# Top-k attention with an ELU network: the scores of a step in one burst over four PSUM banks, with small parts in the banks' corners

## The chip, the core and the metric

The kernel runs on one core of a Trainium2 chip. The metric is the device time of one execution in microseconds (us); lower is better. The engines that matter are TensorE (PE in the profile; PEld are its weight loads), VectorE (DVE), ScalarE (ACT), GpSimd (POOL) and SyncE (SP), which issues the loads and stores. PSUM, where TensorE writes its results, has eight banks of 512 float32 columns.

## The reference

Everything is float32. The shapes are 8 batches, 8 heads, 576 positions, head size 64; the network takes 4608 tokens of 512 values through 2048 hidden units.

```python
scores = scale * np.matmul(q, k.transpose(0, 1, 3, 2))
kth = np.partition(scores, -top_k, axis=-1)[..., -top_k:-top_k + 1]     # top_k = 32
scores = np.where(scores >= kth, scores, -1000000000.0)
attn = np.exp(scores - np.max(scores, axis=-1, keepdims=True))
attn = attn / (np.sum(attn, axis=-1, keepdims=True) + 1e-09)
x = np.matmul(attn, v)            # then (B, H, S, D) -> (B*S, H*D)
h = x @ w_in
g = np.where(h > 0.0, h, np.exp(np.minimum(h, 0.0)) - 1.0)
out = g @ w_out
```

## The kernel before

**Steps.** The attention is cut into 144 steps. A step takes two heads and one tile of 128 queries: 576 = 4 x 128 + 64, so four full tiles for each batch and pair of heads, and the last 64 queries of four heads together as a "rem" tile. The work of a step is spread over four passes of the main loop (line 617). At index n the loop computes the scores of step n + 2 (`scores`, L280), finds the 32 largest of each row of step n on VectorE (`select`, L322: MAX8 and MATCH_REPLACE8, in four parts with a `yield` after each), masks and exponentiates step n - 1 on ScalarE (`mask`, L345), scales it on GpSimd (`normalise`, L362), and transposes step n - 2 on TensorE (`turn`, L375: nine blocks of 128 columns, called as main with four, rest with one and other with four). When the tiles of a group (one, or a pair in most of the run) are transposed, `attend` (L397) multiplies by the values in the next index.

**Scores.** `scores(u, half)` computes half of the 576 keys (HS = 288) for both heads. Head i stands on partitions 64 i to 64 i + 63, so its matmul uses 64 of the 128 rows of TensorE's array. Both heads of one half go to two banks of `ps_sc`, a pool with one buffer, and one ScalarE activation (L297) moves the half to SBUF. The second half is computed later in the same index, with other work between.

**The last 64 keys.** The values of the last 64 positions of two heads share one chunk of 128 partitions (chunk 2 J of `vT`, J = 4). `attend` therefore takes 64 rows for its last chunk, and 128 rows for the four before. Its output has 64 columns of the array per head, so each pair of matmuls stands side by side. `transpose_qk` (L236) turns keys and queries by blocks of 128 positions, and at last the 64 that are left over, with three transposes of 64 rows (L257).

**The network.** `ffn_pieces` (L457) makes pieces: 16 `hidden` pieces for a block of one to three tiles of 128 tokens (L471, then Relu and Exp on ScalarE, L479 and L480, and the gate on VectorE, L451), and four `project` pieces for each tile (L489). `feed` (L577) is called four times in each index; it first puts the open gates on VectorE's list, and then as many pieces on TensorE's as a budget allows. The hidden results and the projections take turns in the pool `ps_f`, three buffers; the transposes and the attend results use `ps_t`, three buffers. With the two banks of `ps_sc` that is all of PSUM.

**Order.** From index 8 on (`tight`) the order of the program is the order in which TensorE, ScalarE, VectorE and GpSimd execute (L643). Before that a scheduler orders the instructions. Each engine takes its list in order and waits by semaphores. Dependences inside one PSUM tile are kept by bank: a write to any part of a bank waits for the reads of that bank which stand ahead of it.

Of the kernel before, what the change touches and what calls it, by code (L numbers as in the profile page):

```python
# [8 lines left out]
AF = mybir.ActivationFunctionType  # L9
ALU = mybir.AluOpType  # L10
FP32 = mybir.dt.float32
U32 = mybir.dt.uint32
I32 = mybir.dt.int32
PSUM = bass.MemoryType.PSUM
# [66 lines left out]
def kernel(  # L81
# [9 lines left out]
    nc = tc.nc  # L91
    P = nc.NUM_PARTITIONS
    B, H, S, D = q.shape
    dm, dff = moe_w_in.shape[0], moe_w_in.shape[1] // 2
    J = S // P
    JP = J * P
    R = S - JP
    HS = S // 2
# [5 lines left out]
    KEYS, QUERIES = R, R + S  # L104
    scale = 1.0 / float(D) ** 0.5
# [3 lines left out]
    def pool(name, bufs, **kw):  # L109
        return ctx.enter_context(tc.tile_pool(name=name, bufs=bufs, **kw))  # L110

    const = pool("const", 1)
    ldpool = pool("ld", 2)
    kvpool = pool("kv", 5)
    scpool = pool("sc", 5)
# [4 lines left out]
    fpool = pool("f", 2)  # L120
    opool = pool("o", 1)
    ps_sc = pool("ps_sc", 1, space=PSUM)
    ps_t = pool("ps_t", 3, space=PSUM)
    ps_f = pool("ps_f", 3, space=PSUM)
    late = {}
    raws = ExitStack()
    early = raws.enter_context(tc.tile_pool(name="early", bufs=1))
# [2 lines left out]
    ident = const.tile([P, P], FP32, tag="ident", name="ident")  # L130
# [78 lines left out]
    loaded, kqT, vT = {}, {}, {}  # L209

    def load_qk(b, hp):
        for name, src in (("k", k), ("q", q)):
            t = ldpool.tile([P, J + 1, 2, D], FP32, tag=name + "in", name=name + "in")
            for hh in range(2):
                nc.sync.dma_start(
                    t[:, 0:J, hh, :],
                    src[b, 2 * hp + hh, 0:JP, :].rearrange("(p j) d -> p j d", j=J),
                )
            nc.sync.dma_start(
                t[0:R, J, :, :],  # L220
                src[b, 2 * hp : 2 * hp + 2, JP:S, :].rearrange("h p d -> p h d"),
            )
            loaded[b, hp, name] = t

    def load_v(b, hp):
        t = kvpool.tile([P, 2 * J + 1, D], FP32, tag="vT", name="vT")
        for hh in range(2):
            h = 2 * hp + hh
            nc.sync.dma_start(
                t[:, hh * J : (hh + 1) * J, :],  # L230
                v[b, h, 0:JP, :].rearrange("(p j) d -> p j d", j=J),
            )
            nc.sync.dma_start(t[hh * R : (hh + 1) * R, 2 * J, :], v[b, h, JP:S, :])
        vT[b, hp] = t

    def transpose_qk(b, hp):  # L236

        d = kvpool.tile([P, 4 * J + 3, D], FP32, tag="kqT", name="kqT")
        kqT[b, hp] = d[:].rearrange("p c d -> p (c d)")
        srcs = [loaded.pop((b, hp, name)) for name in ("k", "q")]
        for i, src in enumerate(srcs):
            ps = ps_t.tile([P, JP], FP32, tag="t", name="qkps")
            for c in range(J):
                nc.tensor.transpose(  # L247
                    ps[:, c * P : (c + 1) * P],
                    src[:, c, :, :].rearrange("p h d -> p (h d)"),
                    ident[:],  # L250
                )
            c0 = KEYS + i * (2 * J + 1) * D
            nc.scalar.copy(kqT[b, hp][:, c0 : c0 + JP], ps[:])
            yield
        ps = ps_t.tile([P, JP], FP32, tag="t", name="qkps")
        for i, src in enumerate((srcs[0], *srcs)):
            nc.tensor.transpose(  # L257
                ps[:, i * R : (i + 1) * R],
                src[0:R, J, :, :].rearrange("p h d -> p (h d)"),
                ident[0:R, 0:R],  # L260
            )
        nc.scalar.copy(
            d[:, 0 : 4 * J + 3 : 2 * J + 1, :],
            ps[:, 0 : 3 * R].rearrange("p (a s) -> p a s", a=3),
        )
        yield

    def start_qk(b, hp):
        turning.append(transpose_qk(b, hp))
# [7 lines left out]

    turning = []

    def scores(u, half):  # L280

        if half == 0:
            u.sc = scpool.tile([P, 2, S], FP32, tag="sc", name="sc")
        ps = ps_sc.tile([P, 2, JP], FP32, tag="s", name="scps")
        q0 = QUERIES + u.t.qt * P
        for h, i, rows in u.heads:
            kq = kqT[u.t.b, h // 2]
            part = slice(i * D, (i + 1) * D)
            k0 = (KEYS if i == 0 else 0) + half * HS
            nc.tensor.matmul(  # L290
                ps[rows, i, 0:HS],
                kq[part, q0 : q0 + u.t.ql],
                kq[part, k0 : k0 + HS],
                start=True,
                stop=True,
            )
        nc.scalar.activation(  # L297
            u.sc[:, :, half * HS : (half + 1) * HS], ps[:, :, 0:HS], AF.Copy, scale=scale
        )

    def select_row(u, i):
        if i == 0:
# [72 lines left out]
    def turn(u, chunks):  # L375

        if u.turned:
            return
        g = u.group
        if g.et is None:  # L380
            g.et = etpool.tile([P, 2 * J + 1, len(g.tiles), P], FP32, tag="et", name="et")
        ps = ps_t.tile([P, JP], FP32, tag="t", name="eps")
        sc = u.sc[:, :, :].rearrange("p i s -> p (i s)")
        n = chunks.stop - chunks.start
        for c in range(n):
            c0 = (chunks.start + c) * P
            nc.tensor.transpose(ps[:, c * P : (c + 1) * P], sc[:, c0 : c0 + P], ident[:])  # L387
        nc.scalar.copy(  # L388
            g.et[:, chunks, u.at, :],
            ps[:, 0 : n * P].rearrange("p (c q) -> p c q", c=n),  # L390
        )
        if chunks.stop == 2 * J + 1:
            u.turned = True
            if u.at == len(g.tiles) - 1:
                closing.append(g)

    def attend(g):  # L397
        t = g.tiles[0]
        ps = ps_t.tile([P, JP], FP32, tag="t", name="avps")
        n = P if t.rem else sum(x.ql for x in g.tiles)  # L400
        for k in range(2 if t.rem else 1):
            hp = 2 * g.hp + k if t.rem else g.hp
            vt = vT[t.b, hp]
            for c in range(J + 1):
                for i in range(2):
                    rows = slice(0, P) if c < J else slice(i * R, (i + 1) * R)
                    chunk = J if c == J else i * (J + 1) + c
                    w = g.et[rows, chunk, :, :].rearrange("p a q -> p (a q)")
                    cols = slice(0, n)
                    if t.rem:  # L410
                        c0 = R * (k if i == 0 else 1 - k)
                        w = w[:, c0 : c0 + R]
                        cols = slice(k * R, (k + 1) * R)
                    nc.tensor.matmul(  # L414
                        ps[i * D : (i + 1) * D, cols],
                        vt[rows, 2 * J if c == J else i * J + c, :],
                        w,
                        start=(c == 0),
                        stop=(c == J),
                    )  # L420
        if t.rem:
            finish(t.block, 2, slice(2 * g.hp, 2 * g.hp + 2), t.cols,
                   ps[:, 0:n].rearrange("p (a q) -> p a q", a=2))
            return
        c0 = 0
        tiles = list(g.tiles)
        while tiles:
            blk, lo, parts = tiles[0].block, tiles[0].cols.start, 0
            while tiles and tiles[0].block is blk:
                parts += 1  # L430
                hi = tiles.pop(0).cols.stop
            finish(blk, parts, g.hp, slice(lo, hi), ps[:, c0 : c0 + hi - lo])
            c0 += hi - lo
# [161 lines left out]
    load_v(0, 0)  # L595
    start_qk(0, 0)
    turn_qk(True)
    scores(steps[0], 0)
    scores(steps[0], 1)
    load_qk(0, 2)  # L600
    start_qk(0, 1)
    turn_qk(True)
    scores(steps[1], 0)
    scores(steps[1], 1)
    load_qk(0, 3)
    for hp in range(1, NHP):
        load_v(0, hp)
# [7 lines left out]
    closing = []  # L615
    main, rest, other = slice(0, J), slice(J, J + 1), slice(J + 1, 2 * J + 1)
    for n in range(NS + 3):
# [2 lines left out]
        ahead, cur, prev, done = step(n + 2), step(n), step(n - 1), step(n - 2)  # L620
        if n < tight:
            turn_qk(True)
            scores(ahead, 0)
            scores(ahead, 1)
            for i in range(2):
                passes = select_row(cur, i)
                next(passes)
                if i == 0:
                    while closing:
                        attend(closing.pop(0))  # L630
                elif prev:
                    normalise(prev)
                    turn(prev, main)
                    turn(prev, rest)
                    turn(prev, other)
                feed(n, 0.25)
                next(passes)
                mask(cur, i)
                feed(n, 0.25)
            continue  # L640
# [4 lines left out]
            )  # L645
        passes = select(cur) if cur else iter(range(4))
        if ahead:
            scores(ahead, 0)
        next(passes)
        feed(n, 0.25)  # L650
        if prev:
            mask(prev, 0)
        turn_qk()
        while closing:
            attend(closing.pop(0))
        if ahead:
            scores(ahead, 1)
        next(passes)
        feed(n, 0.25)
        if done:  # L660
# [49 lines left out]
```

## Time and profile before

| what | value |
|---|---|
| median of 3 runs | 1733.86 us (1732.75 to 1734.05) |
| the profiled execution, its own time | 1732.9 us |
| its span, first to last instruction | 1731.0 us |
| granted TensorE clock, mean | 0.975 |
| busy: PE, DVE, ACT, POOL | 1647.5, 1544.7, 1145.1, 407.5 us |

The profile is read by stretch of time: the share of busy time of each engine in a stretch, what an engine waited for there, and the instructions in order of time with their start. PE's busy time is a union of records that overlap, and includes pauses inside a matmul's record; the distance from the start of one burst of matmuls to the start of the next tells more than the record's length. In the trace one float32 matmul has two MATMUL records (two passes), a transpose one. "128*64" in a row means 128 rows and 64 columns of the array in use, "128x256" the output's partitions and columns of the moving operand.

### The profile page before, as it was taken

How to read it: one execution, taken by the hardware profiler on the slowest of the kernel's cores; microseconds unless marked ns; L12 is line 12 of the kernel's file. 1: busy time of each engine (PE TensorE's matmuls, PEld its weight loads, DVE VectorE, ACT ScalarE, POOL GpSimd, SP SyncE). 2: the span in 40 equal slices, each digit the busy share in tenths (PEclk: the TensorE clock that was granted, in tenths of full speed). 3: DMA queues.
4: the chain of work that ended last, by engine and by line, in shares of the span. 5: the costliest groups of instructions: out<-in, count | busy, mean ns of one | idle time of the engine just before them, and what ended most of it. 6: DMA issues, size and time to landing. Idle time of an engine off the chain costs nothing.

```text
span 1731.0 us, 25867 instructions
## 1 busy us (share of the span) xinstructions
PE 1647.5 (95%) x8592; PEld 1007.8 (58%) x8592; DVE 1544.7 (89%) x3392; ACT 1145.1 (66%) x2509; POOL 407.5 (24%) x1078
## 2 busy tenths in 40 slices
PE   6468999999999999999999999999999999999999
PEld 3245677557474756555456565645547475745565
DVE  6899999999999999999989898999999989997700
ACT  5786787678676867667666675757657585756521
POOL 2674222222222222221212122221222221121100
PEclk9568999999999999999999999999999999999999
DMA  6641021001100110001200111001100000000000
GB/s 155 178 135 44 15 48 34 7 7 42 48 7 7 34 46 23 1 24 31 48 12 1 41 35 34 1 13 42 42 19 1 26 15 27 7 7 7 7 13 12
DMA packets 101125, 56.19 MB, mean 32 GB/s; under 512 B 84096, under 2 KB 92288, under 8 KB 100992
## 3 DMA queue, kind: packets, MB, share of 16 engines
q1 hardware_dynamic: 100992, 54.55, 11.5%
q8 instruction: 67, 1.10, 0.3%
q14 instruction: 66, 0.54, 0.1%
HBM read 45.09 MB, written 9.44 MB: 31 GB/s over the span
## 4 chain that ended last, share of the span: by engine, by line
PE 82%; DVE 8%; ACT 2%; issue 1%; POOL 1%; DMA 0%; ACTq 0%
PE ops L489 28%; PE hps L471 27%; PE avps L414 9%; PE scps L290 9%; PE eps L387 7%; DVE wk L334 3%; DVE m L341 3%; PE qkps L247 1%; DVE m L329 1%; ACT sc L297 1%; DVE gT L451 1%; PE qkps L257 0%; ACT n L480 0%; ACT n L479 0%; DVE wk L311 0%
## 5 line engine op out<-in xcount | busy, mean ns | idle before, releaser
L471 PE MATMUL hps<-xT,w_in 128*128 128x256 f32 (+2 forms) x2432 | 563.7, 378 | 22.8 <-DVE gT L451 15.6
L341 DVE MAX8 m<-wk 128x8 f32<-128x576 f32 x816 | 574.9, 745 | 0.0
L489 PE MATMUL ops<-w_out,gT 128*128 128x512 f32 x1152 | 525.3, 600 | 2.5 <-DVE gT L451 2.5
L471 PEld LDWEIGHTS hps<-xT,w_in 128*128 128x128 f32 x2432 | 406.1, 193 | 143.1 <-DVE gT L451 26.0
L334 DVE MATCH_REPLACE8 wk<-m,wk 128x576 f32<-128x576 f32 x544 | 399.4, 741 | 0.0
L489 PEld LDWEIGHTS ops<-w_out,gT 128*128 128x128 f32 x1152 | 208.7, 190 | 240.4 <-issue 232.5
L367 POOL TENSOR_SCALAR dene<-den 128x2 f32<-128x2 f32 x144 | 33.1, 230 | 1000.2 <-ACT sc L358 999.9
L290 PE MATMUL scps<-kqT 64*128 64x288 f32 (+1 forms) x1280 | 232.4, 462 | 32.6 <-ACT sc L297 24.3
L388 ACT COPY et<-eps 128x512 f32<-128x512 f32 (+1 forms) x432 | 189.8, 474 | 102.4 <-PE eps L387 102.3
L371 POOL TENSOR_SCALAR sc<-sc,rec 128x576 f32<-128x576 f32 x288 | 213.9, 752 | 185.1 <-DVE rec L369 175.2
L357 ACT ACTIVATE sc<-sc,neg 128x576 f32<-128x576 f32 x288 | 224.0, 778 | 48.4 <-POOL neg L354 48.1
L297 ACT ACTIVATE sc<-scps 128x576 f32<-128x576 f32 x288 | 185.9, 646 | 86.2 <-PE scps L290 81.4
L358 ACT ACTIVATE sc<-sc,gap 128x576 f32<-128x576 f32 x288 | 223.1, 775 | 25.3
L479 ACT ACTIVATE n<-hps 128x256 f32<-128x256 f32 (+2 forms) x304 | 111.5, 367 | 144.9 <-PE hps L471 131.9
L387 PEld LDWEIGHTS eps<-ident,sc 128*128 128x128 f32 x1296 | 156.8, 144 | 84.6 <-issue 53.9
L414 PE MATMUL avps<-et,vT 128*64 128x256 f32 (+5 forms) x2080 | 200.4, 328 | 3.8 <-ACT et L388 3.7
L387 PE MATMUL eps<-ident,sc 128*128 128x128 f32 x1296 | 192.1, 282 | 12.3 <-POOL sc L371 11.7
L334 DVE MATCH_REPLACE8 wk<-m,sc 128x576 f32<-128x576 f32 x272 | 199.7, 741 | 0.0
L329 DVE MAX8 m<-sc 128x8 f32<-128x576 f32 x272 | 191.1, 744 | 0.0
L451 DVE SCALAR_TENSOR_TENSOR gT<-n,hps 128x256 f32<-128x256 f32 (+2 forms) x304 | 117.6, 391 | 71.4 <-ACT n L480 70.7
L414 PEld LDWEIGHTS avps<-et,vT 128*64 128x64 f32 (+1 forms) x2080 | 115.4, 138 | 95.0 <-issue 53.8
L290 PEld LDWEIGHTS scps<-kqT 64*128 64x128 f32 (+1 forms) x1280 | 91.5, 180 | 126.0 <-issue 47.9
(40 smaller groups left out, 840.8 us busy)
## 6 DMA issues: line engine op xcount, KB each, us to landing
kin<-in_k_dram SPq DMA_DIRECT2D x64, 128.0 KB, 2.8
qin<-in_q_dram SPq DMA_DIRECT2D x64, 128.0 KB, 2.9
raw<-in_moe_w_in_dram SPq DMA_DIRECT2D x16, 512.0 KB, 4.1
vT<-in_v_dram SPq DMA_DIRECT2D x64, 128.0 KB, 2.3
raw<-in_moe_w_out_dram SPq DMA_DIRECT2D x16, 512.0 KB, 3.3
out_dram<-osb SPq DMA_DIRECT2D x32, 256.0 KB, 2.2
kin<-in_k_dram SPq DMA_DIRECT2D x32, 32.0 KB, 2.5
qin<-in_q_dram SPq DMA_DIRECT2D x32, 32.0 KB, 2.5
```

Source lines behind the costliest of these rows:

```text
L290: nc.tensor.matmul(ps[rows, i, 0:HS], kq[part, q0 : q0 + u.t.ql], kq[part, k0 : k0 + HS], start=True, stop=True,)
L297: nc.scalar.activation(u.sc[:, :, half * HS : (half + 1) * HS], ps[:, :, 0:HS], AF.Copy, scale=scale)
L329: nc.vector.max(found[i], cur[i])
L334: nc.vector.match_replace(wk[i], found[i], cur[i], TAKEN)
L341: nc.vector.max(found[i], cur[i])
L357: nc.scalar.activation(sc, sc, AF.Prelu, bias=neg[:], alpha=STEEP)
L358: nc.scalar.activation(sc, sc, AF.Exp, bias=gap[:], accum_out=u.den[:, i : i + 1])
L371: nc.gpsimd.tensor_scalar(u.sc[:, i, :], u.sc[:, i, :], rec[:, i : i + 1], 1.0, ALU.mult, ALU.mult)
L387: nc.tensor.transpose(ps[:, c * P : (c + 1) * P], sc[:, c0 : c0 + P], ident[:])
L414: nc.tensor.matmul(ps[i * D : (i + 1) * D, cols], vt[rows, 2 * J if c == J else i * J + c, :], w, start=(c == 0), stop=(c == J),)
L471: nc.tensor.matmul(ps[:, 0:n_tok], w_in[:, i, f * P : (f + 1) * P], blk.xT[:, i, 0:n_tok], start=(i == 0), stop=(i == NC - 1),)
L489: nc.tensor.matmul(blk.o[:], blk.gT[f // NG][:, f % NG, s * P : (s + 1) * P], w_out[:, f, :], start=(f == 0), stop=(f == NF - 1),)
```

## The change

`ps_sc` now holds one tile, `wide`, of four banks, allocated once. `ps_t` and `ps_f` go from three buffers to two. `scores(u)` issues the four matmuls of a step one after the other, head i and half h to bank 2 i + h, and then two activations, one for each head. In the banks' last 224 columns, which the scores leave free, stand the single block `rest` of `turn` (bank 3) and the left-over keys and queries (bank 1). The left-over 64 keys and 64 queries of two heads are loaded into one chunk of the `kin` tile, keys on partitions 0 to 63 and queries on 64 to 127; two transposes of all 128 rows, the second shifted by 64 columns, leave keys, keys and queries in 192 columns. They come first in `transpose_qk`. The last values of each head get a chunk of their own, with zeros (a GpSimd memset for each head) on the other head's partitions, so that `attend` takes 128 rows throughout. In the main loop `attend` stands right behind `scores`, ahead of the first `feed`.

```diff
-    ps_t = pool("ps_t", 3, space=PSUM)
-    ps_f = pool("ps_f", 3, space=PSUM)
+    ps_t = pool("ps_t", 2, space=PSUM)
+    ps_f = pool("ps_f", 2, space=PSUM)
+    wide = ps_sc.tile([P, 4, JP], FP32, tag="s", name="scps")
...
     def load_qk(b, hp):
...
-                t[0:R, J, :, :],
+                last[0:R, J, :, :] if name == "k" else last[R:P, J, :, :],
...
     def load_v(b, hp):
-        t = kvpool.tile([P, 2 * J + 1, D], FP32, tag="vT", name="vT")
+        t = kvpool.tile([P, 2 * J + 2, D], FP32, tag="vT", name="vT")
...
-            nc.sync.dma_start(t[hh * R : (hh + 1) * R, 2 * J, :], v[b, h, JP:S, :])
+            mine = slice(hh * R, (hh + 1) * R)
+            other = slice((1 - hh) * R, (2 - hh) * R)
+            nc.gpsimd.memset(t[other, 2 * J + hh, :], 0.0)
+            nc.sync.dma_start(t[mine, 2 * J + hh, :], v[b, h, JP:S, :])
...
     def transpose_qk(b, hp):
...
+        ps = wide[:, 1, HS : HS + 3 * R]
+        for i in range(2):
+            nc.tensor.transpose(
+                ps[:, i * R : i * R + P],
+                srcs[0][:, J, :, :].rearrange("p h d -> p (h d)"),
+                ident[:],
+            )
+        nc.scalar.copy(
+            d[:, 0 : 4 * J + 3 : 2 * J + 1, :],
+            ps.rearrange("p (a s) -> p a s", a=3),
+        )
         for i, src in enumerate(srcs):
...
-        for i, src in enumerate((srcs[0], *srcs)):
-            nc.tensor.transpose(
-                ps[:, i * R : (i + 1) * R],
-                src[0:R, J, :, :].rearrange("p h d -> p (h d)"),
-                ident[0:R, 0:R],
-            )
...
-    def scores(u, half):
+    def scores(u):
...
+        for half in range(2):
+            for h, i, rows in u.heads:
+                kq = kqT[u.t.b, h // 2]
+                part = slice(i * D, (i + 1) * D)
+                k0 = (KEYS if i == 0 else 0) + half * HS
+                nc.tensor.matmul(
+                    wide[rows, 2 * i + half, 0:HS],
+                    kq[part, q0 : q0 + u.t.ql],
+                    kq[part, k0 : k0 + HS],
+                    start=True,
+                    stop=True,
+                )
+        for i in range(2):
+            nc.scalar.activation(
+                u.sc[:, i, :].rearrange("p (a s) -> p a s", a=2),
+                wide[:, 2 * i : 2 * i + 2, 0:HS], AF.Copy, scale=scale,
+            )
...
     def turn(u, chunks):
-        ps = ps_t.tile([P, JP], FP32, tag="t", name="eps")
+        if chunks.stop - chunks.start == 1:
+            ps = wide[:, 3, HS : HS + P]
+        else:
+            ps = ps_t.tile([P, JP], FP32, tag="t", name="eps")
...
     def attend(g):
-                    rows = slice(0, P) if c < J else slice(i * R, (i + 1) * R)
-                    w = g.et[rows, chunk, :, :].rearrange("p a q -> p (a q)")
+                    w = g.et[:, chunk, :, :].rearrange("p a q -> p (a q)")
...
-                        vt[rows, 2 * J if c == J else i * J + c, :],
+                        vt[:, 2 * J + i if c == J else i * J + c, :],
...
         if ahead:
-            scores(ahead, 0)
+            scores(ahead)
+        while closing:
+            attend(closing.pop(0))
         next(passes)
         feed(n, 0.25)
         if prev:
             mask(prev, 0)
         turn_qk()
-        while closing:
-            attend(closing.pop(0))
-        if ahead:
-            scores(ahead, 1)
         next(passes)
```

More of the change, by code (lines that the diff above doesn't have):

```diff
@@ L212, in load_qk @@
         for name, src in (("k", k), ("q", q)):
-            t = ldpool.tile([P, J + 1, 2, D], FP32, tag=name + "in", name=name + "in")
+            n = J + 1 if name == "k" else J
+            t = ldpool.tile([P, n, 2, D], FP32, tag=name + "in", name=name + "in")
+            if name == "k":
+                last = t
             for hh in range(2):
@@ L254, in transpose_qk @@
             yield
-        ps = ps_t.tile([P, JP], FP32, tag="t", name="qkps")
-        for i, src in enumerate((srcs[0], *srcs)):
-            nc.tensor.transpose(
-                ps[:, i * R : (i + 1) * R],
-                src[0:R, J, :, :].rearrange("p h d -> p (h d)"),
-                ident[0:R, 0:R],
-            )
[L262 to L266, printed above, removed]
     def start_qk(b, hp):
@@ L278 @@
     turning = []
-    def scores(u, half):
-        if half == 0:
-            u.sc = scpool.tile([P, 2, S], FP32, tag="sc", name="sc")
-        ps = ps_sc.tile([P, 2, JP], FP32, tag="s", name="scps")
+    def scores(u):
+        u.sc = scpool.tile([P, 2, S], FP32, tag="sc", name="sc")
         q0 = QUERIES + u.t.qt * P
[L286 to L295, printed above, removed]
-            )
-        nc.scalar.activation(
-            u.sc[:, :, half * HS : (half + 1) * HS], ps[:, :, 0:HS], AF.Copy, scale=scale
-        )
+        for half in range(2):
[14 more added lines that the diff above has]
+                wide[:, 2 * i : 2 * i + 2, 0:HS], AF.Copy, scale=scale,
+            )
     def select_row(u, i):
@@ L597 @@
     turn_qk(True)
-    scores(steps[0], 0)
-    scores(steps[0], 1)
+    scores(steps[0])
     load_qk(0, 2)
@@ L602 @@
     turn_qk(True)
-    scores(steps[1], 0)
-    scores(steps[1], 1)
+    scores(steps[1])
     load_qk(0, 3)
@@ L647 @@
         if ahead:
-            scores(ahead, 0)
+            scores(ahead)
+        while closing:
+            attend(closing.pop(0))
         next(passes)
@@ L653 @@
         turn_qk()
-        while closing:
-            attend(closing.pop(0))
-        if ahead:
-            scores(ahead, 1)
         next(passes)
```

## The prediction

> **What bounds the kernel now.** I read busy time by stretch first, because an average over the span hides which engine leads where.
>
> ```profile
> core 0: us, PE busy (x) PEld busy (x) DVE busy (x) ACT busy (x) POOL busy (x), PEclk, DMA share, GB/s
> 200.00:400.00 200.00, 191.68 (x1341) 129.14 (x1341) 198.11 (x459) 145.34 (x351) 46.26 (x139) 1.00 0.10 26
> 400.00:600.00 200.00, 197.94 (x1009) 123.70 (x1006) 198.11 (x438) 143.63 (x313) 44.66 (x133) 1.00 0.11 27
> 600.00:800.00 200.00, 197.86 (x1062) 119.13 (x1060) 194.63 (x428) 136.76 (x296) 44.64 (x133) 1.00 0.09 25
> 800.00:1000.00 200.00, 199.79 (x953) 116.30 (x953) 186.55 (x409) 134.52 (x285) 42.34 (x127) 1.00 0.10 26
> 1636.00:1731.00 95.00, 91.07 (x320) 53.16 (x318) 7.07 (x18) 22.81 (x52) 3.82 (x9) 0.99 0.04 14
> ```
>
> Up to 600 us VectorE is busy 99% and bounds the kernel. From 800 us it is at 93% and TensorE at nearly 100%. After 1636 us only network work is left. Then what VectorE waited for, first from 200 to 600 us, then from 600 to 1636 us:
>
> ```profile
> DVE rec L369 <- POOL dene L367: 2.9, 4, 1.2
> DVE gT L451 <- ACT n L480: 0.9, 3, 0.5
> ```
>
> ```profile
> DVE rec L369 <- POOL dene L367: 44.9, 28, 3.9
> DVE gT L451 <- ACT n L480: 23.2, 26, 2.6
> ```
>
> So 3.8 us can be gained from 200 to 600, and at most 68 us after it. TensorE's own waits after 600 are small (the scores' wait for L297 is the largest, 6.5 us), so there TensorE executes its list without pause, and the list's length is the time. Third, TensorE's bursts in order of time (start, record length):
>
> ```profile
> 1019.70 1.89 PE L471 MATMUL hps<-xT,w_in 128*128 128x256 f32 x8
> 1021.52 0.76 PE L290 MATMUL scps<-kqT 64*128 64x288 f32 x4
> 1022.21 1.99 PE L471 MATMUL hps<-xT,w_in 128*128 128x256 f32 x8
> 1024.13 2.53 PE L414 MATMUL avps<-et,vT 128*64 128x256 f32 x20
> 1026.59 0.76 PE L290 MATMUL scps<-kqT 64*128 64x288 f32 x4
> 1027.28 1.99 PE L471 MATMUL hps<-xT,w_in 128*128 128x256 f32 x8
> 1029.11 1.15 PE L387 MATMUL eps<-ident,sc 128*128 128x128 f32 x9
> ```
>
> Read from start to start. Eight passes of 384 columns with no change around them run from 814.66 to 817.24 us, 0.84 us per 1000 columns: 0.215 for 256, 0.241 for 288; two passes on different rows or columns of the array run side by side. The score burst is two such pairs, 0.48, but takes 0.69. The hidden piece is 8 x 0.215 = 1.72, but takes 1.82 with a change of array shape at its end, 1.83 with one ahead of it, 1.92 with both. The attend burst (ten pairs, 2.15) takes 2.46 with a change ahead, one inside (its last four records are 64*64) and one at its end. So **each change of the rows or columns in use costs 0.093 us, and the first full-width matmul after it another 0.10 (0.05 for 64 columns)**, since the weights of the pass behind it aren't loaded ahead across the change.
>
> **What the Trainium skill says.** "TensorEngine Tiling (Array Packing)", Key Properties: changing the tiling mode drains TensorE. The trace agrees, with 0.093 us for the drain and the exposed weight load on top. "PSUM — Partial Sum Buffer", on bank collisions: TensorE's writes and another engine's reads are to be kept apart by bank and quadrant, even at different columns. So parts in a score bank's corner wait for that bank's activation, and the next scores for the corner's copy; no run here shows the corner. "TensorE: Matmul & The Clock Gate", Part 3: matmuls in different row groups run concurrently; the trace agrees (a pair of score passes starts 0.005 us apart).
>
> **The change part by part.**
>
> *Fewer shape changes.* I counted the places in TensorE's program order where the shape changes: 744 before, 384 after. An index with attend had six (into and out of the first half; into attend, into its 64-row chunk, into the second half, out); it now has three. One without had four, now two. The padded chunk costs no time: its pairs are still side by side at 0.215. Three transposes of 64 columns become two of 128: 0.17 to 0.22 us, 32 times, +1.6 in all. By stretch of 16 steps, from step 48 (its transposes begin at 590.7 us): 482 changes become 242. 240 x 0.093 = 22.3. The exposed weight loads fall from 35.4 to 20.7, so 14.7. Less 0.6 for the transposes: 36.4 us of TensorE's list, namely 6.8, 5.6, 7.4, 4.7, 6.9 for steps 48 to 127 and 5.0 for the rest. The same prices added up over the list before give 181.6 us for steps 80 to 95, and the trace has 180.7, so they hold. The 18 us saved ahead of step 48 are worth nothing: VectorE has 1 to 2 us in 200 to give.
>
> *How much of it arrives.* In steps 48 to 63 VectorE's waits (5.4 us idle from 600 to 800) let me count 4 of 6.8: **33.6**.
>
> *One burst instead of two halves.* The second half's wait for the single buffer goes: of the 6.5 us above I take **5**. In its place: the corner of bank 1, used directly behind the scores with no piece between in 4 of the 20 cases after step 48. It waits for the first activation, 0.65 (L297) plus ScalarE's usual delay of 0.05 to 0.4: **-4**. The corner of bank 3 comes at least 2.6 us behind the scores, both activations take 1.3: nothing, but up to 1.5 each where ScalarE is behind by a mask (0.78 + 0.78 + 0.19).
>
> *Attend earlier.* It now stands behind scores instead of behind scores and a piece, so it could meet the copy of "other" (L388). That copy ends 1.9 us (median, at most 2.9) after its transposes from 700 us on; attend comes 2.3 us or more after them. Nothing. But the first piece now has 2.3 us of attend ahead of it, and its gate is due one VectorE pass earlier than that of the piece which stood there (at 807.09 the gate waited 1.56 us). VectorE may fall back behind TensorE by up to about 1.9 us before GpSimd's scaling delays the transposes (in the index at 809.47, scaling ends at 812.14 and the transposes begin at 814.06), so I count little: as the two engines come within 3 to 4% of each other, **-6** (1 us per 16 steps, 0 to 15).
>
> *Two buffers for ps_f.* For each piece I compared its start with the end of the gate two allocations earlier. From 800 us on, three pieces in each 200 us start ahead of it, by 1.4 us in total: nothing. From 200 to 400 us, 30 of 57 do, by 37 us in total, since TensorE runs ahead there. That is idle time of TensorE, unless the piece's gate then comes late for VectorE. With the piece's own latency to the end of Exp (1.72 us for 128 columns, 2.77 for 256), ten gates from 110 to 400 us come late, by 3.4 us together: **-3.4**. If ScalarE's backlog stayed as it was, instead of absorbing the delay, it would be 13.2 from 200 to 400 and 30.8 before: 44 is the upper end.
>
> *The rest.* ps_t with two buffers: rest and left-over no longer use it. Copies end about 1 us after main, 1.9 after other, pieces of 1.8 us and more stand between: nothing. The 64 memsets (0.2 us each by the profile's one memset, 128x128) lie on GpSimd, 24% busy; those that wait for an attend stand an index or more behind it, and what queues behind them is neg and gap, due after a VectorE pass. Nothing, up to 2. At the start the first transposes now wait for the queries' tail (landing at 6.65 us, where keys began at 4.74), but ScalarE can't copy before 9.72, so nothing; with the scheduler's new order up to step 8, -5 to +5.
>
> Sum: 33.6 + 5 - 4 - 6 - 3.4 = 25.2. The span goes from 1731.0 to 1705.8. The profiled execution's own time is 1.9 above its span and 1.0 below the median shown: 1708.7, so **1709**.
>
> **Rivals.** *More arrives* (12%): VectorE keeps up without loss and no corner waits: 36.4 + 6.5 = 43, 1691. For it: VectorE had 68 us to give. Against: it is above 93% everywhere. *The gate takes the saving* (12%): VectorE can't fall back, so the 1.7 us that the first gate waits in an attend index come each time (45 after step 48); it then repeats what the later gate's 1.56 us cost before, and a gain of 0 to 8 stays: 1726 to 1734. Against: the 1.9 us of room. *Two gate buffers starve VectorE* (10%, the slower side): between 110 and 400 us, where VectorE bounds, each delayed piece hands its delay on. With 44 instead of 3.4: 25.2 - 40.6 = -15, 1749. It decides from 29 us lost there on. For it: a median margin of -0.14 us from 200 to 400. Against: the gates had 1.3 us of median slack behind Exp. That the change doesn't do what it says is excluded by the order of its instructions: four score matmuls stand together in every step.
>
> **Numbers.** Forecast 66%, own range 1698 to 1722. A measurement of this kernel tells 0.2% (3.5 us) from no change. Faster: 66 + 12 + 6 = 84%; within 0.2%: 4%; slower: 12%. The range reaches down into the first rival and up to the middle of the second: 1692 to 1729.
>
> **What would show it.** Right: from 800 us on VectorE's share at 96 to 97%, its wait for dene shrunk to a third; score bursts of about 1.17 us (0.10 + 4 x 0.241 + 0.09), attend 2.3; no 64*64 row at L414 for full tiles; index times as before up to 600 us. Wrong: gates waiting above 40 us for Exp after 600, TensorE waiting over 10 us for activations of the scores or for L451 there, or VectorE below 96% between 200 and 400 us.

## The result, and the profile after

The changed kernel takes 1747.97 us (median of 4 runs, 1745.18 to 1748.35) against 1733.53: ratio 1.008, 95% interval 1.0063 to 1.0098. It is slower by 14 us (0.8%); 1709 was predicted. Its profiled execution has a span of 1745.9 us. In the rows of the changed kernel L297 is the scores' matmul and L305 their activation, L255 and L260 the left-over keys' transposes and their copy, L399 the transposes of `turn`, L425 `attend`, and L482, L491 and L462 the hidden piece, its Exp and its gate.

Busy time by stretch of the changed kernel, with the columns of the table before:

```profile
core 0: us, PE busy (x) PEld busy (x) DVE busy (x) ACT busy (x) POOL busy (x), PEclk, DMA share, GB/s
200.00:400.00 200.00, 178.58 (x1275) 123.92 (x1274) 186.82 (x429) 136.35 (x333) 43.71 (x135) 0.99 0.09 24
400.00:600.00 200.00, 186.16 (x940) 121.06 (x938) 192.10 (x424) 136.59 (x296) 45.60 (x140) 1.00 0.09 24
600.00:800.00 200.00, 191.93 (x1109) 124.58 (x1110) 195.71 (x433) 138.96 (x305) 45.83 (x141) 1.00 0.10 27
800.00:1000.00 200.00, 194.09 (x913) 116.46 (x913) 188.83 (x412) 132.63 (x279) 43.48 (x134) 1.00 0.09 24
```

Up to 600 us neither engine is full any more: VectorE fell from 99% to 93 and 96%, TensorE too. After 800 us TensorE has idle time (97%), and VectorE is at 94%, hardly above the 93% of before. What VectorE waited for in the changed kernel, from 200 to 600 us and then from 600 to 1636 (total, times, longest), and TensorE's waits in the second stretch:

```profile
DVE gT L462 <- ACT n L491: 14.1, 22, 2.1
DVE rec L378 <- POOL dene L376: 6.9, 5, 1.8
```

```profile
DVE gT L462 <- ACT n L491: 31.3, 39, 2.3
DVE rec L378 <- POOL dene L376: 28.8, 18, 3.1
```

```profile
PE hps L482 <- DVE gT L462: 15.7, 25, 1.8
PE scps L399 <- ACT kqT L260: 8.7, 5, 2.0
PE scps L255 <- ACT sc L305: 5.3, 4, 1.4
```

Where VectorE bounds, its waits rose from 3.8 to 21.0 us. Where TensorE bounds, three waits are new, 29.7 us together: a piece for a gate, the rest block for the copy of the left-over keys, and the left-over keys for the scores' activation. The wait of 6.5 us that the scores had for their single buffer is gone. The start of each step's selection dates the loss: step 16 begins 3.4 us later than before (234.0 against 230.6), step 48 20.1 us later (583.9 against 563.8), and the last selection ends 13.7 us later (1649.4 against 1635.7). So 20 us are lost ahead of step 48, and of the 28.6 us expected behind it (33.6 + 5 - 4 - 6) 6.4 arrive.

The bursts themselves came out as worked out. TensorE's list in order of time (start, record length):

```profile
1042.56 1.24 PE L297 MATMUL scps<-kqT 64*128 64x288 f32 x8
1043.73 2.38 PE L425 MATMUL avps<-et,vT 128*64 128x256 f32 x20
1046.04 3.72 PE L482 MATMUL hps<-xT,w_in 128*128 128x256 f32 x16
```

From start to start the scores take 1.17 us and attend 2.31, as the prediction's last part has them.

### The profile page after: what moved, and what is told of

It is laid out like the page before. It is cut to its first block, busy times and chain, and to the rows that moved or that the text cites. A ratio compares the mean times of both kernels' runs of the same rounds, so it can differ in the third digit from the quotient of the medians.

```text
span 1745.9 us, 26194 instructions
## 1 busy us (share of the span) xinstructions
PE 1603.1 (92%) x8560; PEld 1030.3 (59%) x8560; DVE 1546.0 (89%) x3392; ACT 1142.8 (65%) x2509; POOL 416.6 (24%) x1142
## 3 DMA queue, kind: packets, MB, share of 16 engines
q1 hardware_dynamic: 100992, 54.55, 11.3%
## 4 chain that ended last, share of the span: by engine, by line
PE 62%; DVE 26%; ACT 6%; issue 3%; POOL 2%; DMA 1%; SPq 0%; ACTq 0%; POOLq 0%
PE ops L500 25%; PE hps L482 17%; DVE wk L343 10%; DVE m L350 8%; PE avps L425 8%; PE scps L297 6%; PE eps L399 4%; DVE m L338 2%; DVE gT L462 2%; ACT sc L366 1%; ACT sc L367 1%; DVE m L326 1%; DVE wk L320 1%; PE qkps L267 1%; ACT n L491 1%
## 5 line engine op out<-in xcount | busy, mean ns | idle before, releaser
L482 PE MATMUL hps<-xT,w_in 128*128 128x256 f32 (+2 forms) x2432 | 563.3, 380 | 69.4 <-DVE gT L462 60.4
L482 PEld LDWEIGHTS hps<-xT,w_in 128*128 128x128 f32 x2432 | 411.2, 194 | 182.5 <-DVE gT L462 87.4
L305 ACT ACTIVATE sc<-scps 128x576 f32<-128x576 f32 x288 | 171.6, 647 | 99.2 <-PE scps L297 98.1
L400 ACT COPY et<-eps 128x512 f32<-128x512 f32 x288 | 165.1, 573 | 90.5 <-PE eps L399 90.4
L462 DVE SCALAR_TENSOR_TENSOR gT<-n,hps 128x256 f32<-128x256 f32 (+2 forms) x304 | 119.1, 395 | 95.7 <-ACT n L491 95.7
L425 PE MATMUL avps<-et,vT 128*64 128x256 f32 (+2 forms) x2080 | 186.6, 324 | 12.7 <-ACT et L400 12.5
L297 PE MATMUL scps<-kqT 64*128 64x288 f32 (+1 forms) x1280 | 187.4, 442 | 9.0 <-ACT kqT L273 4.6
L399 PEld LDWEIGHTS eps<-ident,sc 128*128 128x128 f32 x1152 | 145.5, 145 | 80.4 <-issue 51.3
L399 PE MATMUL eps<-ident,sc 128*128 128x128 f32 x1152 | 177.4, 280 | 13.3 <-POOL sc L380 13.2
L425 PEld LDWEIGHTS avps<-et,vT 128*64 128x64 f32 x2080 | 119.1, 140 | 84.0 <-issue 29.9
L297 PEld LDWEIGHTS scps<-kqT 64*128 64x128 f32 (+1 forms) x1280 | 100.9, 183 | 74.6 <-issue 29.9
```

Source lines behind the costliest of these rows:

```text
L297: nc.tensor.matmul(wide[rows, 2 * i + half, 0:HS], kq[part, q0 : q0 + u.t.ql], kq[part, k0 : k0 + HS], start=True, stop=True,)
L305: nc.scalar.activation(u.sc[:, i, :].rearrange("p (a s) -> p a s", a=2), wide[:, 2 * i : 2 * i + 2, 0:HS], AF.Copy, scale=scale,)
L425: nc.tensor.matmul(ps[i * D : (i + 1) * D, cols], vt[:, 2 * J + i if c == J else i * J + c, :], w, start=(c == 0), stop=(c == J),)
L482: nc.tensor.matmul(ps[:, 0:n_tok], w_in[:, i, f * P : (f + 1) * P], blk.xT[:, i, 0:n_tok], start=(i == 0), stop=(i == NC - 1),)
```

## The experiments

**Two buffers for the gates alone**, in the kernel before.

```diff
-    ps_f = pool("ps_f", 3, space=PSUM)
+    ps_f = pool("ps_f", 2, space=PSUM)
```

> The kernel before with two buffers instead of three for the hidden and projection results (ps_f), nothing else. Theory of the buffers (TensorE's pieces wait for VectorE's gate two pieces back, and the next gate then comes late for VectorE): 1748 to 1760 us, slower by 14 us or more, with VectorE waiting more than 10 us for Exp between 200 and 600 us where it waited 0.9. Theory of the early attend (two buffers cost little, the moved attend is what makes gates late): within 5 us of 1733.5.

Measured: 1761.04 us, ratio 1.0158 (1.0143 to 1.0174), 27 us slower. From index 8 on TensorE's program order is unchanged, so this is waiting alone. VectorE's wait for Exp from 200 to 600 us rose from 0.9 to 6.5 us, less than the 10 expected, that for dene from 2.9 to 7.5. Step 48 begins 16.0 us later than before (579.8 against 563.8); the other 10.9 us up to the last selection are lost behind it. How a wait comes about, TensorE and then VectorE of this run:

```profile
300.85 1.16 PE L471 MATMUL hps<-xT,w_in 128*128 128x128 f32 x8 [0.23 <-DVE gT L451]
301.84 0.60 PE L387 MATMUL eps<-ident,sc 128*128 128x128 f32 x4
302.28 1.06 PE L471 MATMUL hps<-xT,w_in 128*128 128x128 f32 x8
304.14 1.16 PE L471 MATMUL hps<-xT,w_in 128*128 128x128 f32 x8 [0.80 <-DVE gT L451]
305.23 0.76 PE L290 MATMUL scps<-kqT 64*128 64x288 f32 x4
```

```profile
303.81 0.27 DVE L451 SCALAR_TENSOR_TENSOR gT<-n,hps 128x128 f32<-128x128 f32 x1
304.00 1.42 DVE L329 MAX8 m<-sc 128x8 f32<-128x576 f32 x2
305.33 0.27 DVE L451 SCALAR_TENSOR_TENSOR gT<-n,hps 128x128 f32<-128x128 f32 x1
305.99 0.29 DVE L451 SCALAR_TENSOR_TENSOR gT<-n,hps 128x128 f32<-128x128 f32 x1 [0.39 <-ACT n L480]
```

The piece at 304.14 needs the buffer of the piece at 300.85, whose gate VectorE reaches at 303.81, behind its MAX8 and MATCH_REPLACE8. TensorE idles 0.80, the scores behind the piece start later as well, and VectorE then waits 0.39 at 305.99 for that piece's own Exp. A wait for dene comes by a longer way, here with lines left out between:

```profile
279.69 0.76 ACT L388 COPY et<-eps 128x512 f32<-128x512 f32 x2 [3.40 <-PE eps L387]
281.20 0.77 ACT L358 ACTIVATE sc<-sc,gap 128x576 f32<-128x576 f32 x1
282.42 0.17 DVE L369 RECIPROCAL rec<-dene 128x2 f32<-128x2 f32 x1 [1.37 <-POOL dene L367]
```

ScalarE stands 3.40 us for TensorE's transposes; only behind their copies come the two masks, whose sums dene needs, and VectorE stands 1.37 us for it. The kernel before has such waits too; what the missing buffer adds is the rise from 2.9 to 7.5. The theory of the buffers stands.

**Two buffers for the transposes alone** (`ps_t` 3 to 2, kernel before).

> The kernel before with two buffers instead of three for transposes and attend results (ps_t), nothing else. Here rest and the left-over keys still use this pool, which the changed kernel takes out of it. Both theories: 1733 to 1740 us; the copies end one to two us after their transposes and further work stands between. If it is 10 us slower or more, neither theory is complete.

Measured: 1782.79 us, ratio 1.0282 (1.0267 to 1.0298): 49 us slower, a miss. TensorE's waits from 600 us on have a row that neither the kernel before nor the changed one has:

```profile
PE eps L387 <- ACT et L388: 21.4, 31, 1.1
```

Main, rest and other follow each other in this pool; with two buffers, other waits for main's copy. With the 5.2 us from 200 to 600 the row comes to 26.6 us; what makes up the rest of the 49 I did not follow. In the changed kernel rest stands in a corner and the row is absent, so this isn't its loss. It suggests what the corners are good for; two buffers without corners in the changed kernel were not run.

**Attend earlier alone.**

```diff
         if ahead:
             scores(ahead, 0)
+        while closing:
+            attend(closing.pop(0))
         next(passes)
...
         turn_qk()
-        while closing:
-            attend(closing.pop(0))
         if ahead:
             scores(ahead, 1)
```

> The kernel before with attend moved directly behind the first half of the scores, ahead of the first piece; all buffers as before. Theory of the early attend: slower by 10 us or more, with VectorE's wait for Exp well above the 24 us of before. Theory of the buffers: the same as before or a little faster (one shape change fewer in an index with attend, some 45 times after 600 us at 0.2 us: up to 9 us), 1724 to 1735 us.

Measured: 1752.38 us, ratio 1.011 (1.0093 to 1.0127), 18 us slower with all buffers as before. The sign and size are those of the theory of the attend, but VectorE's wait for Exp rises only between 200 and 600 us (0.9 to 8.2); after 600 its wait for dene rises (45.2 to 51.4). An index of this run from the first stretch, TensorE and then VectorE:

```profile
489.28 2.53 PE L414 MATMUL avps<-et,vT 128*64 128x256 f32 x20
491.74 1.99 PE L471 MATMUL hps<-xT,w_in 128*128 128x256 f32 x8
```

```profile
491.36 1.41 DVE L341 MAX8 m<-wk 128x8 f32<-128x576 f32 x2
494.63 0.42 DVE L451 SCALAR_TENSOR_TENSOR gT<-n,hps 128x256 f32<-128x256 f32 x1 [1.86 <-ACT n L480]
```

The first piece starts only at 491.74, behind attend's 2.46 us. Its gate is due behind the second pass, at 492.77, and starts at 494.63: VectorE stands for 1.86 us. Attend itself also met the copy of "other": TensorE waited there for L388, 4.3 us from 200 to 600 and 2.6 after, where the kernel before has no such wait from 200 us on. Step 48 begins 9.0 us later than before (572.8 against 563.8), and the stretch from there to the last selection is 8.6 us longer. Both theories are right, each about one part.

**The padded values alone.** The changed lines of `load_v` and `attend`, kernel before.

> The kernel before with the padded last values alone (no 64-row chunk in attend). Both theories: the shape change inside the attend burst goes (about 0.15 us, of which TensorE bounds some 45 bursts after 600 us), the burst takes 2.3 instead of 2.46 us: 1725 to 1731 us.

Measured: 1719.72 us, ratio 0.992 (0.9906 to 0.9935), 14 us faster, more than expected: both theories had counted too few changes. The trace has 637 in place of 744, and 72 of the 107 lie from step 48 to the last selection. At 0.093 + 0.05 each they are worth 10.3 us there, and that stretch is 10.4 us shorter (1061.5 against 1071.9). So the price of a shape change holds. 3.8 us of the gain stand at step 48 already (560.0 against 563.8), where the prediction had nothing; 2.5 of them come ahead of step 16.

**Attend put back in the changed kernel** (behind `turn_qk()`).

> The changed kernel with attend put back to its old place behind the first piece and the key transposes; all else as changed. If the costs of the parts add (two gate buffers +27 and early attend +18 us, each measured alone), it falls by 18 us less 56 more shape changes (some 8 us): 1735 to 1742 us. If the two gate buffers alone set the time and the place of attend matters only with three: 1746 to 1752 us.

Measured: 1723.48 us, ratio to before 0.9948 (0.9933 to 0.9963): 24.5 us faster than the changed kernel, and faster than either theory had it (18 less 8 was the larger gain expected), although the list has 56 shape changes more.

**The gate's buffer freed by ScalarE**, in the changed kernel; the copy stands ahead of the Exp, and `fpool` has three buffers.

```diff
-            gates.append((blk.gT[f // NG][:, f % NG, 0:n_tok], n, ps))
+            dst = blk.gT[f // NG][:, f % NG, 0:n_tok]
+            nc.scalar.copy(dst, ps[:, 0:n_tok])
+            gates.append((dst, n, dst))
```

> The changed kernel with the hidden results copied by ScalarE from PSUM into the gate's own place in SBUF, where the gate then works in place, and a third buffer for the Exp values: a PSUM buffer comes free behind ScalarE and no longer behind VectorE's gate. ScalarE gets 304 copies of about 0.37 us, 112 us more on 65%. Theory of the buffers: 1748 less about 27, 1716 to 1730 us, and TensorE's wait for the gate is gone. Theory that attend's place alone costs: 1743 us or more.

Measured: 1718.56 us, ratio 0.9914 (0.9898 to 0.9931): 29 us faster than the changed kernel. After 600 us TensorE's wait for a buffer of ps_f falls from 15.7 to 0.2 us; between 200 and 600 it falls from 25.8 to 11.3, now for ScalarE's copy, so there it is not gone. A third buffer of ps_f, which would be the plain test, does not fit beside the four score banks. VectorE's gates did not become faster: the 304 take 130.9 us in all, 120.1 in the changed kernel.

**Both repairs.**

> The changed kernel with both: hidden results copied by ScalarE, and attend at its old place. If the two causes are all that stands against the shorter list of TensorE: 1700 to 1715 us, near the 1709 of the prediction. If a further cause is missing (corners, ScalarE's load): above 1720 us.

Measured: 1706.18 us, ratio 0.9846 (0.9832 to 0.9861), within the expected range. That this is near the predicted 1709 is luck and no proof of the prediction's sum: with attend back this kernel has 56 shape changes more than the changed one, and the experiment with the score banks, further down, shows a further cause.

**The first half moved next to attend** (kernel before with padding; in an index with attend `scores(ahead, 0)` and attend stand behind `mask(prev, 0)`, and `turn_qk()` behind the second half).

> The kernel before with the padded values and, in an index with attend, the first half of the scores moved behind the first piece so that attend stands between the two halves (halves, buffers and corners as before): one shape change fewer in each such index than with padding alone (637 to 605). If only TensorE's list counts: 1713 to 1718 us against 1719.7 of padding alone. If moving work past a piece delays VectorE as the early attend did: 1722 us or more.

Measured: 1772.26 us, ratio 1.0225 (1.021 to 1.024): 53 us slower than padding alone, for 32 shape changes saved. TensorE's waits after 600 us show why; with padding alone this row has 6.5 us (from 200 to 600 it has 24.0 here and 2.2 there):

```profile
PE scps L293 <- ACT sc L300: 34.8, 41, 2.4
```

The first half's activation now stands behind the mask's two activations on ScalarE's list, and the second half waits for it.

**The score banks as two tiles**, on top of both repairs; the other changed lines only follow the new names:

```diff
-    wide = ps_sc.tile([P, 4, JP], FP32, tag="s", name="scps")
+    wide = [ps_sc.tile([P, 2, JP], FP32, tag=f"s{i}", name=f"scps{i}") for i in range(2)]
```

> As the changed kernel with hidden results copied by ScalarE and attend at its old place, and the score banks as two tiles of two banks, one for each head, so that the rest block (bank 3) need not wait for the left-over keys' copy (bank 1). There TensorE waited 4.4 us for that copy after 600 us, and 4.0 between 200 and 600. If that wait is on the path: 1700 to 1704 us against 1706.2; if VectorE's room hides it: 1705 to 1708.

Measured: 1694.44 us, ratio 0.9779 (0.9764 to 0.9793), 12 us faster than with the repairs alone, more than the 2 to 6 expected, and the fastest version here. VectorE's waits from 200 to 600 us, from 600 to 1636, and TensorE's largest wait in the second stretch:

```profile
DVE rec L380 <- POOL dene L378: 2.2, 1, 2.2
DVE gT L464 <- ACT n L495: 1.0, 2, 0.6
```

```profile
DVE rec L380 <- POOL dene L378: 27.8, 13, 13.6
DVE gT L464 <- ACT n L495: 13.3, 18, 2.0
```

```profile
PE scps L257 <- ACT sc L307: 2.2, 3, 0.7
```

The rest block's wait for the left-over keys' copy is gone, though the two stood in different banks before as well. The left-over keys' own wait fell too, from 5.2 to 2.2 us after 600. In one tile each of these waits was 1.3 us there and ended when the activations of both heads had ended; in two tiles it is 0.74 and ends with the first head's, which alone reads bank 1. The section on the kernel says that dependences inside a tile are kept by bank; for the wide tile that was not so in either place: the wait went by the whole tile. VectorE's waits after 600 us are 41.1 us in all, but 13.6 of these come behind the last selection; the other 27.5 stand against 68.1 in the kernel before.

**The left-over keys between the two main transposes**, on top of that.

> The same, and the left-over transposes moved from directly behind the scores to between the two main transposes of keys and queries: their wait for the first score activation (5.2 us after 600, 6.7 between 200 and 600) should go. If on the path: 1695 to 1702 us; the next scores may then wait for the left-over copy instead, which would leave it at 1702 to 1708.

Measured: 1709.62 us, ratio 0.9868 (0.9853 to 0.9882), 15 us slower than without. The second of the two expected outcomes came, and larger: the next scores need the corner's bank, and wait for its copy after 600 us:

```profile
PE scps L300 <- ACT kqT L264: 16.5, 17, 1.5
```

**Padding with the gate freed**, three buffers.

> The kernel before (halves, three gate buffers, attend in its place) with the padded values and with the hidden results copied by ScalarE. Theory of the buffers: three buffers already keep TensorE from waiting much for a gate (8.0 us between 200 and 600 with padding alone), so little changes against 1719.7: 1712 to 1722 us, 304 copies on ScalarE included. If freeing the gate gains by something else than the missing third buffer, it gains here as much as in the changed kernel, 25 us or more: below 1697 us.

Measured: 1729.51 us, ratio 0.9976 (0.9968 to 0.9983), 10 us slower than padding alone. Step 16 begins at 236.8 instead of 228.1 us, and steps 16 to 48 take as long as with padding alone (331.6 and 331.9 us). So where three buffers exist, freeing the gate gains nothing. This run has the copies, the third buffer of `fpool` and the gate in SBUF as well, and together they gain nothing here, which speaks against them as the source of the 29 us in the changed kernel.

Of the 8.7 us lost ahead of step 16, 7.3 are VectorE's own gates: 35 of them take 16.9 us there, against 9.6 with padding alone. A gate of this run with GpSimd's addition beside it (L183, from the decoding of the weights), then the same pair with padding alone, where one input of the gate is in PSUM:

```profile
115.25 1.20 DVE L453 SCALAR_TENSOR_TENSOR gT<-n,gT 128x128 f32<-128x128 f32 x1
115.04 1.26 POOL L183 TENSOR_TENSOR w_out<-raw 128x512 int32<-128x512 int32 x1
```

```profile
120.51 0.28 DVE L453 SCALAR_TENSOR_TENSOR gT<-n,hps 128x128 f32<-128x128 f32 x1
120.31 1.27 POOL L183 TENSOR_TENSOR w_out<-raw 128x512 int32<-128x512 int32 x1
```

Nine gates of this run take 0.91 to 1.36 us ahead of step 16. Each of them starts while such an addition runs and ends about 0.15 us after it; the other 26 take 0.26 to 0.35.

**The gate on PSUM again**, attend put back and two tiles.

> The changed kernel with attend at its old place and the score banks as two tiles, but the gate still reading PSUM, so that a buffer of ps_f waits for VectorE. If two gate buffers cost about what they did with attend put back alone (1723.5 to 1706.2, 17 us): 1708 to 1714 us against 1694.4 with the gate freed. If the split has already taken most of that wait away: below 1702 us, and then this is the better version, without ScalarE's copies.

Measured: 1712.78 us, ratio 0.9883 (0.9866 to 0.9899), within the first range: two gate buffers still cost 18 us against the freed gate.

## Why the prediction was wrong

From the changed kernel to the fastest version the steps are: attend put back, 1747.97 to 1723.48 (-24.5); two tiles, to 1712.78 (-10.7); gate freed, to 1694.44 (-18.3). Together -53.5 us.

- **Fewer shape changes: right, with less arriving.** From step 48 to the end of the selections the changed kernel has 242 changes, as counted. That stretch, less the waits listed for TensorE in it, is about 30 us shorter than before (1065.5 - 31.2 against 1071.9 - 7.7); the prediction had 36.4, and what became of the other 6 is not shown. Padding alone brought what its changes are worth. In the fastest version the stretch takes 39.6 us less than before (1599.4 - 567.1 against 1635.7 - 563.8). The prediction had 33.6 for the shorter list and 5 for the half's wait, but this kernel has 37 more changes there than the changed one, and VectorE waits less in it, so the nearness is no check of the two terms. Up to step 48 the fastest version gained nothing, as the cap by VectorE has it; padding alone gained 3.8 there, 1.3 of it between steps 16 and 48.
- **"Two buffers for ps_f ... -3.4": the step that failed most.** It measured 27 us alone, 29 in the changed kernel, and 18 once attend and corners were mended. Of the 27, 16.0 were lost by step 48, where the prediction had 3.4, and 10.9 behind it, where it had nothing. I had compared each piece with the gate two allocations back in the old trace, one piece at a time, let ScalarE's backlog absorb the delay, and called TensorE's pause idle time. But everything behind the piece on TensorE's list shifts with it: scores and transposes at once, and through the copies the masks on ScalarE's list, whose result VectorE's reciprocal needs. The wait for dene, which the step left out, rose with the wait for Exp in the first experiment.
- **"Attend earlier ... -6 (0 to 15)": right behind step 48, missing ahead of it.** It measured 18 us alone, 24.5 in the changed kernel, and 12.4 where the gate was freed. I had placed the whole term after 600 us. In the experiment with attend alone 8.6 us are lost behind step 48, inside the stated range, and 9.0 ahead of it, where I had nothing: up to 600 us VectorE bounds, so a gate wait of 1.86 us as in that trace is not paid back, and the room of 1.9 us by which VectorE could fall back is of no use. "Nothing" for the copy of "other" was wrong as well: in that experiment TensorE waited for it 6.9 us from 200 us on.
- **"The corner of bank 3 ... nothing": wrong.** I only looked at the scores' activations. Within one tile the rest block also waited for the left-over keys' copy, which stands behind a mask on ScalarE. For bank 1 the prediction had a wait for the first activation, -4; it was for both, 5.3 us after 600 and 3.9 from 200 to 600. Two tiles gain 10.7 to 11.7 us by both waits together; how much each is worth was not measured.
- **The rival on the slower side** had 1749 and the mechanism of the gate buffers. The time matches by luck, the account does not: of the 53.5 us the gate buffers carried 34 to 55%, and the early attend 23 to 46%.
- Of the signs named for a wrong prediction two came: VectorE below 96% between 200 and 400 us (93%), and TensorE waiting over 10 us for the gates after 600 (15.7). Of the signs for a right one the bursts of scores and attend came (1.17 and 2.31 us), VectorE's share of 96 to 97% after 800 us did not (94%).
- The waits that overlap cannot be added: alone the two parts cost 27 and 18 us, and mending them together with the corners gained 53.5. The split between them depends on the order in which they are mended.
- Two readings in the prediction are off, and nothing rests on them. Most pairs of score passes start 0.006 to 0.007 us apart, not 0.005. VectorE is not above 93% everywhere: from 1400 to 1600 us it is at 91% (182.3 of 200 us).

## What to carry to other kernels

A saving on the bounding engine's list is worth its price per change only if what pays for it, here PSUM buffers, does not tie that engine to the next one: with two engines at 91% and above, one buffer fewer for the hidden results cost 18 to 29 us, about what 240 drains (22 us) had saved. The part that needed no buffer, the padding, was worth 14 us alone. Asking of each delayed instruction only whether its own consumer is late is not enough; everything behind it in the same queue is delayed too. And small parts put in the corner of a tile that another engine reads may inherit its waits, so separate tiles are worth trying before a new layout.

## What the runs showed of the hardware

In the stretch where VectorE bounds, TensorE's pauses reached VectorE about in full: the run with two gate buffers has 10 us more of waits for gates on TensorE from 200 to 600 us (16.6 against 6.4), and VectorE's own waits in that stretch rise by 10.2 (3.8 to 14.0). Copies on ScalarE, with the engine 73 to 75% busy from 200 to 600 us in the fastest version (145.6 and 150.0 us of 200), did not make VectorE wait there: 3.2 us in all. A VectorE gate of 128x128 with both inputs in SBUF took up to 1.36 us when it started beside GpSimd's addition, where the same gate with one input in PSUM took 0.26 to 0.29 beside it.
